# Attention beside a long convolution on one core: V projected in two halves of the heads, half-time transfers in four pieces, the last normalisation in two halves, later k chunks issued by SyncE

## The chip, the cores and the metric

The kernel runs on one core of a Trainium2 chip. The metric is the device time of one execution in microseconds (us); the times shown are of separate executions of the same program. The engines are TensorE (PE in the profile; PEld is its weight loads), VectorE (DVE), ScalarE (ACT), GpSimd (POOL) and SyncE (SP), which here only issues transfers.

## The reference

Two computations stand side by side in the output's 1024 columns. All tensors are bfloat16, the sequence has 2048 rows.

```python
# A: 32 heads of 16, columns 0..511 of the output
qkv = x @ wqkv                                   # [2048,512] @ [512,1536]
p   = softmax((q @ k^T) * 16**-0.5)              # no mask
a   = (p @ v).reshape(2048, 512) @ wo
# B: columns 512..1023
k_shift[s] = sum over t of k[s-3+t] * shift_k[:, 3-t]      # 4 taps
kv  = k_shift * v
y   = causal convolution of kv along s with ssm_k (2048 taps a channel) + kv * ssm_D
b   = q * y
```

## The kernel before, in words

**Attention.** Scores are made transposed, a block at a time: one block is one head strip, 128 keys by 512 queries. There are 2048 blocks: 4 query blocks `qb` x 8 groups `g` of four heads x 16 key tiles `kt` x 4 strips `s`. A step T takes a chunk of two or three blocks: TensorE makes them in two or three of six PSUM banks, three banks to even steps and three to odd ones (`emit_qk`, the L791 matmuls, K tile `KTo` and masked Q `QT`), ScalarE takes the exponential of the whole chunk in one instruction into `PT` (L798, 128x1024 for a pair, 128x1536 for a triple). In some triples the third block goes to VectorE instead (`exp_on_dve`: L817, a linear pass by GpSimd at L290, three passes at L826 and L827, result in `PTD`), and ScalarE then gets two blocks. Two steps later TensorE multiplies the exponentials with V (`emit_pv`, L866, four strips side by side). V lies in `VAF` with two columns of ones beside each head of 16, so that the sums come out with the product. After 64 blocks a group is done: `finish_group` transposes the PSUM bank on VectorE (L892), takes reciprocals (L899), multiplies (L901), and after every second group transposes back into `OTN` (L907). The output projection (`op_out`, L940) follows, 128 rows at a time.

**Projections.** x is transposed on TensorE (`turn_x`, L485), Q, K and V come from `pe_unit` (L507, L514, L521; a unit is four matmuls of 512 columns into one PSUM bank) and are copied out on VectorE by `evac_unit` (L542 for Q, L552 for K, L558 for V). In the first 70 steps the table `early` says at which step each unit comes; after that `units` does, by the group that needs the unit first (`next_unit`). A step with such a unit takes only two blocks, since the unit uses the third bank of its step. All 16 V units stand in `early`, all 32 heads at once, one key tile each.

**Convolution.** `kv_chunk` makes kv on VectorE for 256 rows at a time, chunk 7 first and chunk 0 last; `load_kv` fetches for each chunk v and four shifted copies of k (m = 0 to 3). v and m = 3 are issued by SyncE, m = 0, 1, 2 by GpSimd. Chunk 0 has rows before the sequence's start: GpSimd zeroes three partitions first (L424), and the shifted copies are fetched in two transfers each, the first of 127, 126 and 125 rows. When chunk 0 is done `start_conv` lets the convolution begin: 512 channels, four at a time (`qd`), 64 small matmuls for each four (`conv_lags`, L998), against a band matrix that SyncE fetches from a scratch buffer, 512 KB a channel, into a ring of 14 slots (`load_wr`). After each 32 channels `conv_turn` transposes back and multiplies by q in `QN`. `QN` holds 256 of the 512 channels: at half-time (after `conv_turn` 7) it is stored in one transfer of 1 MB and, 14 steps later, filled again with the second half of q in one transfer of 1 MB. Both are in SyncE's queue among the band matrices.

**What sets the order.** All engines run fixed streams of instructions, written when the program is built. A planner in Python keeps an estimated clock for each engine: PE's stream is written step by step (`emit_qk`, a unit, `emit_pv`, then early units or convolution up to an estimated limit), VectorE's from a list of jobs with due times (`dve_job`, `commit_one`), the transfers by estimated landing times (`landing`, `due_in`, `DMA_NS`). Matmuls with no result (`keep_busy`, `keep_zero`, `keep_active`: L1180, L1191, L1120) are put where the planner sees room and too little work in the past 3.4 us (`WINDOW`, `ACTIVE`). At run time each engine takes its stream in order and waits on semaphores.

**The end.** After the last exponential come the last L866, `finish_group`, four L940 into four banks, and `op_out_end`: ScalarE copies rows t = 1 and 3 and issues their stores, VectorE copies t = 0 and 2, whose stores SyncE issues.

## Time and profile before

| | |
|---|---|
| median of three executions | 843.6 us (839.74 to 861.82) |
| the profiled execution | 842.7 us |
| its span, first to last instruction | 840.8 us |
| mean granted TensorE clock | 0.993 |
| busy: ACT / DVE / PE / POOL | 818.2 / 797.5 / 710.1 / 283.7 us |
| moved by the DMA engines | 295.68 MB, 352 GB/s on average |

The profiled execution's own time is 1.9 us more than its span and 0.9 us below the median. A row of the timeline merges neighbouring instructions of one kind: start, length of the merged stretch, engine, line, count, and in brackets how long the engine stood idle before it and what ended that. SPq, ACTq and POOLq rows are the issuing of transfers. Two activations in a row overlap in the profile, so the mean length of one instruction is more than its share of the stretch.

### The profile page before, as it was taken

To read this page: it belongs to the slowest core of one execution; us is meant where nothing else is said; L and a number is where in the kernel's file an instruction comes from. 1 tells how busy PE (TensorE), PEld (TensorE's weight loads), DVE (VectorE), ACT (ScalarE), POOL (GpSimd) and SP (SyncE) were. 2 spreads that over 40 slices of the span, in tenths; PEclk is the share of its full clock that TensorE was granted. 3 is DMA by queue.
4 is the path that set the end of the run, shared out by engine and by line. 5 is a ranking of instruction groups with operands and counts; after the bars stand their busy time and mean duration, and the time that the engine had idled before them with its cause. 6 is when DMAs were issued, how large, how long until landed. Compare 5 with 4: busy or idle time off the path is not lost.

```text
span 840.8 us, 29871 instructions
## 1 busy us (share of the span) xinstructions
PE 710.1 (84%) x13098; PEld 310.1 (37%) x13144; DVE 797.5 (95%) x1346; ACT 818.2 (97%) x732; POOL 283.7 (34%) x307
## 2 busy tenths in 40 slices
PE   8988888888888888888888888788888888888887
PEld 3322333433333333333333334333333443333332
DVE  3998899999999999999999999999999999999996
ACT  6998999999999999999999999999999999999997
POOL 3232233333333333333332423333333333333331
PEclk9999999999999999999999999999999999999899
DMA  9878699999999999999998999999999999999810
GB/s 325 304 247 304 206 408 357 381 408 404 380 357 405 378 410 396 375 386 384 380 380 312 380 394 408 367 398 389 368 368 356 387 411 402 359 398 380 336 51 26
DMA packets 95778, 295.68 MB, mean 352 GB/s; under 512 B 11173, under 2 KB 27554, under 8 KB 95394
## 3 DMA queue, kind: packets, MB, share of 16 engines
q1 hardware_dynamic: 91266, 285.25, 89.5%
q0 software_dynamic: 2240, 7.34, 2.6%
q8 instruction: 105, 1.72, 0.8%
q10 hardware_dynamic: 2144, 1.18, 0.5%
q14 instruction: 23, 0.19, 0.1%
HBM read 287.31 MB, written 6.42 MB: 349 GB/s over the span
## 4 chain that ended last, share of the span: by engine, by line
ACT 72%; DVE 14%; PE 9%; issue 2%; DMA 1%; POOL 1%; ACTq 0%; DVEq 0%
ACT PT L798 72%; PE PS L791 3%; DVE EI L817 3%; DVE PTD L827 2%; DVE EM L826 2%; PE PS L866 2%; DVE WKV L826 2%; PE PS L521 1%; DMA WKV<-in_A_wqkv_dram 1%; PE PS L998 1%; DVE DT L892 1%; PE PS L507 1%; PE PS L514 1%; PE PS L940 1%; DMA QT<-in_B_k_dram 0%
## 5 line engine op out<-in xcount | busy, mean ns | idle before, releaser
L798 ACT ACTIVATE PT<-PS 128x1024 bf16<-128x1024 f32 (+1 forms) x726 | 814.6, 1338 | 11.1 <-PE PS L791 9.5
L791 PE MATMUL PS<-QT,KTo 32*128 32x512 bf16 x2048 | 286.5, 386 | 113.0 <-ACT PT L798 94.9
L998 PE MATMUL PS<-WR,KVP 128*30 128x128 bf16 (+15 forms) x8192 | 257.3, 221 | 2.7 <-issue 2.5
L290 POOL TENSOR_SCALAR EM<-EI 128x512 f32<-128x512 uint16 x131 | 129.2, 986 | 243.8 <-DVE WKV L826 122.4
L290 POOL TENSOR_SCALAR WKV<-EI 128x512 f32<-128x512 uint16 x130 | 128.2, 986 | 235.0 <-DVE EM L826 106.9
L998 PEld LDWEIGHTS PS<-WR,KVP 128*30 128x30 bf16 (+15 forms) x8192 | 177.9, 95 | 77.5 <-issue 37.7
L866 PE MATMUL PS<-PT,VAF 128*32 128x512 bf16 x1787 | 187.7, 392 | 1.3 <-DVE VAF L558 0.5
L817 DVE TENSOR_SCALAR EI<-PS 128x512 int32<-128x512 f32 x261 | 177.8, 681 | 3.4 <-PE PS L791 3.3
L826 DVE SCALAR_TENSOR_TENSOR EM<-EM 128x512 f32<-128x512 f32 x262 | 175.0, 683 | 1.8 <-POOL EM L290 1.5
L826 DVE SCALAR_TENSOR_TENSOR WKV<-WKV 128x512 f32<-128x512 f32 x260 | 173.1, 682 | 0.2
L791 PEld LDWEIGHTS PS<-QT,KTo 32*128 32x128 bf16 x2048 | 71.7, 91 | 274.7 <-ACT PT L798 223.8
L827 DVE SCALAR_TENSOR_TENSOR PTD<-EI,EM 128x512 uint16<-128x512 int32 x131 | 89.0, 680 | 0.4
L827 DVE SCALAR_TENSOR_TENSOR PTD<-EI,WKV 128x512 uint16<-128x512 int32 x130 | 88.1, 679 | 0.3
L866 PEld LDWEIGHTS PS<-PT,VAF 128*32 128x32 bf16 x1787 | 47.3, 93 | 106.7 <-issue 96.4
L866 PE MATMUL PS<-PTD,VAF 128*32 128x512 bf16 x261 | 78.5, 390 | 0.2
L1120 PE MATMUL PS<-IDN,ZER 128*32 128x512 bf16 x396 | 43.8, 380 | 0.0
L892 DVE STREAM_TRANSPOSE DT<-PS 128x512 f32<-128x512 f32 x31 | 22.2, 715 | 8.4 <-PE PS L866 8.1
L866 PEld LDWEIGHTS PS<-PTD,VAF 128*32 128x32 bf16 x261 | 19.8, 95 | 19.5 <-issue 8.6
L542 DVE TENSOR_TENSOR QT<-PS,MSK 128x1024 bf16<-128x1024 f32 x15 | 18.4, 1224 | 4.4 <-PE PS L507 4.3
L367 POOL DMA_DIRECT2D WR<-in_B_k_dram x15 | 11.0, 736 | 23.3 <-DVE KVP L618 14.7
L521 PE MATMUL PS<-WKV,xT 128*128 128x512 bf16 x58 | 17.8, 383 | 1.0 <-issue 0.8
L558 DVE CAST VAF<-PS 128x512 bf16<-128x512 f32 x16 | 11.0, 689 | 7.1 <-PE PS L521 7.1
(77 smaller groups left out, 272.3 us busy)
## 6 DMA issues: line engine op xcount, KB each, us to landing
WR<-kz_scratch SPq DMA_DIRECT2D x512, 512.0 KB, 7.9
WR<-in_B_k_dram POOLq DMA_DIRECT2D x15, 256.0 KB, 7.2
kz_scratch<-WR SPq DMA_DIRECT2D x4, 544.0 KB, 6.7
out_dram<-QN SPq DMA_DIRECT2D x2, 1024.0 KB, 7.5
QT<-in_B_k_dram POOLq DMA_DIRECT2D x7, 256.0 KB, 6.5
out_dram<-OUTA SPq DMA_DIRECT2D x12, 128.0 KB, 6.4
WR<-in_B_v_dram SPq DMA_DIRECT2D x5, 256.0 KB, 8.8
WR<-in_B_k_dram SPq DMA_DIRECT2D x5, 256.0 KB, 12.1
```

The costliest lines, as they stand in the source:

```text
L290: q.h = pool.op(lambda e: e.tensor_scalar(UB[m % len(UB)], f, PA, PB, ALU.mult, ALU.add), [h, fx.h, free], cost=Beside((h[0], h[1] + 1)))
L521: return e.matmul(PS[:, bank, :], lhsT=xT[:, dc, kt * 128:(kt + 1) * 128], rhs=WV[:, dc, :], start=(dc == 0), stop=(dc == 3))
L542: hh = dve_job(lambda e: e.tensor_tensor(QT[:, qb % 2, 2 * o:2 * o + 2, :], src, MSK[:, :, 0:1].broadcast_to([128, 2, QB]), ALU.mult), [h, ...
L791: ins = e.matmul(PS[:, bank, :], lhsT=KTo[32 * s:32 * s + 32, g // 2, kt * 128:(kt + 1) * 128], rhs=QT[32 * s:32 * s + 32, qb % 2, g, :], ...
L798: h_exp[T] = act.op(lambda e: e.activation(PT[:, T % R_PT, 0:n * QB], PS[:, banks[0]:banks[0] + n, :].rearrange("p b f -> p (b f)"), ACT.E ...
L817: h_fix[i] = job(lambda e: e.tensor_scalar(ei, PS[:, bank, :], FIX_LO, FIX_ADD, ALU.max, ALU.add), [h, h_pair.get(i - 4)], 692.0, end)
L826: js.append(job(lambda e, c=c: e.scalar_tensor_tensor(u, u, c, u, ALU.add, ALU.mult), [js[-1]], 693.0, due + 700.0 * (len(js) - 3)))
L827: js.append(job(lambda e: e.scalar_tensor_tensor(PTD[:, i % 4, :].bitcast(UINT16), ei, 2.0 ** -9, u, ALU.mult, ALU.add), [js[2], (lambda: ...
L866: ins = e.matmul(PS[32 * s:32 * s + 32, pvb(qb * NG + g), :], lhsT=VAF[:, kt, h * VW:h * VW + 32], rhs=rhs, start=first[b], stop=last[b], ...
L892: h_t = dve_job(lambda e: e.transpose(out=dt, in_=PS[:, pvb(n), :]), [h, h_mult.get(n - 2 if n == 2 else n - 1) if n != 1 else None], 717. ...
L998: ins = e.matmul(PS[32 * c:32 * c + m * NB - n, BGB, 128 * kk:128 * kk + 128], lhsT=KVP[:, o:o + 4 * (m * NB - n) - 3:4], rhs=WR[:, d % R_ ...
L1120: ins = e.matmul(PS[32 * s:32 * s + 32, pvb(n), :], lhsT=ZER[:, 0:32], rhs=IDN[:, :].rearrange("p (a f) -> p a f", a=1).broadcast_to([128, ...
```

## The change

- **V in halves.** A V unit now covers two key tiles and half of the heads: eight matmuls of 256 columns instead of four of 512, one copy of the same size. `VAF` holds the two halves of a key tile 304 columns apart. The weights come in two transfers; the second half's go into `OUTA`, which is free until the first output projection (whose copy now waits for the last V matmul). Of the 16 units, the eight of the first half and two of the second stand in `early`, six of the second in `units`; the K units (1,2) and (1,3) go from `units` into `early`.
- **Fill.** `keep_busy` reads the identity instead of `VAF`, so it can run from the start, and its bound in the early steps is `EARLY_ACTIVE` 6000 instead of 4800.
- **Half-time in pieces.** The store of `QN` and its refilling become four transfers of 256 KB each, four steps apart, and the planner charges 1000 ns for each instead of 8000 ns in one place.
- **Last normalisation in halves.** `finish_half` does columns 0 to 255 through all its passes, then 256 to 511. In `op_out_end` ScalarE copies t = 0, 1, 3 and VectorE t = 2; SyncE issues the stores of t = 0, 1, 2.
- **k chunks by SyncE.** For chunks 4 to 0 all of k is issued by SyncE. The zeroed area of chunk 0 is half as large. The planner reckons chunk 0's landing 3 us later.

```diff
+VHALF = 304
+VROW = 2 * VHALF
+EARLY_ACTIVE = 6000.0
+KV0_NS = 6600.0
+QN_STEPS = 4
+QN_NS = 1000.0
...
-    WV = WKV[:, 1, :, :]
+    WV = [WKV[:, 1, :, 0:256], OUTA[:, 0:2, :].rearrange("p a (b d) -> p (a b) d", d=256)]
...
-    h_wv = landing(dma(act, d_w[2], WV, wview[:, :, 2 * D:3 * D]), 8.5)
+    h_wv = [landing(dma(act, d_w[2], WV[0], wview[:, :, 2 * D:2 * D + 256]), 8.5)]
...
+    h_wv.append(landing(dma(act, d_w[5], WV[1], wview[:, :, 2 * D + 256:3 * D]), 14.5))
...
-            z = QT[0:3, 1, 2:8, :]
+            z = QT[0:3, 1, 2:8:2, :]
...
-            q = sp if m == 3 else pool
+            q = sp if m == 3 or j < 5 else pool
...
-            due_in(h_kv[(j, 0)], at_of(deps[0] if deps[0] and j else h_kvfree[2] if not j else h_edge), 3600.0)
+            due_in(h_kv[(j, 0)], at_of(deps[0] if deps[0] and j else h_kvfree[2] if not j else h_edge), 3600.0 if j else KV0_NS)
...
+            _, f, i = u
+            deps += h_x[i // 2] + [h_wv[f]]
...
             def mm(e, dc):
-                return e.matmul(PS[:, bank, :], lhsT=xT[:, dc, kt * 128:(kt + 1) * 128], rhs=WV[:, dc, :],
-                                start=(dc == 0), stop=(dc == 3))
+                for c in (2 * dc % 4, 2 * dc % 4 + 1):
+                    kt = 2 * i + dc // 2
+                    ins = e.matmul(PS[:, bank, 256 * (dc // 2):256 * (dc // 2) + 256], lhsT=xT[:, c, kt * 128:(kt + 1) * 128],
+                                   rhs=WV[f][:, c, :], start=(c == 0), stop=(c == 3))
...
+    def finish_half(p, c, h):
+        cols = slice(256 * c, 256 * c + 256)
+        dt, dtn = DT[:, cols], DTN[:, p % 2, cols]
+        h_t = dve_job(lambda e: e.transpose(out=dt, in_=PS[:, pvb(n), cols]), [h, h_mult[n - 1]], 400.0, 300.0 + c)
...
+        h_r = dve_job(lambda e: e.reciprocal(rcp, blocks[:, :, DH:DH + 1]), [h_t], 170.0, 0.0)
...
+        for i in range(2):
+            t = 2 * c + i
+            h_otn[(p, t + 1)] = h_otn[p] = dve_job(
+                lambda e, t=t: e.transpose(out=OTN[:, oslot(n), 128 * t:128 * t + 128], in_=DTN[:, p % 2, 128 * t:128 * t + 128]),
...
+        if last:
+            for c in range(2):
+                finish_half(p, c, h)
+            return
...
-        if t % 2:
+        if t != 2:
             hh = act.op(lambda e: e.activation(dst, PS[:, bank, :], ACT.Copy), [h], cost=515.0)
...
-        dma(act if t % 2 else sp, d_outE, out2[r0:r0 + 128, 0:D], dst, [hh])
+        dma(act if t == 3 else sp, d_outE, out2[r0:r0 + 128, 0:D], dst, [hh])
...
-            ho = dma(sp, d_outB[0], dst, QN[:, :, :], [hh])
-            if sl == 0:
-                dve_later.append((len(chunks) + 14, lambda: load_qn(1, [ho], 0, NB)))
+            def part(i):
+                ho[i] = dma(sp, d_outB[i], dst[:, 4 * i:4 * i + 4, :], QN[:, 4 * i:4 * i + 4, :], [hh])
+                later_row(QN_NS)
+            def again(i):
+                load_qn(1, [ho[i]], 4 * i, 4 * i + 4, i == 3)
+                later_row(QN_NS)
...
-    early = {1: ("v", 0), 3: ("v", 1), 5: ("t", 3), 6: ("v", 2), 8: ("t", 2), 9: ("v", 3), 10: ("k", 0, 1),
+    early = [(0, ("r",)), (1, ("v", 0, 0)), (2, ("x", 1, 0)), (4, ("x", 1, 1)), (6, ("t", 3)), (7, ("v", 0, 1)), (9, ("t", 2)),
...
-    units = [(2 + 8 / 16, ("k", 1, 2)), (2 + 12 / 16, ("k", 1, 3))]
+    units = []
...
+    units += [(4 + i / 8, ("v", 1, i)) for i in range(2, 8)]
...
-            ins = e.matmul(PS[:, bank, :], lhsT=IDN[:, :], rhs=VAF[:, 0, 0:512], start=True, stop=True)
+            ins = e.matmul(PS[:, bank, :], lhsT=IDN[:, :], rhs=IDN[:, :].rearrange("p (a f) -> p a f", a=1).broadcast_to([128, 4, 128]),
+                           start=True, stop=True)
```

Three places show what moves. First TensorE's stream some ten steps into the program, before. QT,KTo is a chunk's scores, WKV,xT half a V unit, PT,VAF the product with V, IDN,KVP a transposition of x, IDN,SHK a spread of the shift taps:

```order
L791 MATMUL PS<-QT,KTo 128x512 x2
L866 MATMUL PS<-PT,VAF 32x512 x4
L485 MATMUL PS<-IDN,KVP 128x128 x8
L791 MATMUL PS<-QT,KTo 128x512 x2
L521 MATMUL PS<-WKV,xT 128x512 x2
L791 MATMUL PS<-QT,KTo 128x512 x2
L866 MATMUL PS<-PT,VAF 32x512 x4
L521 MATMUL PS<-WKV,xT 128x512 x2
L791 MATMUL PS<-QT,KTo 128x512 x2
L485 MATMUL PS<-IDN,KVP 128x128 x8
```

The same place of the changed kernel, where L806 is the scores, L881 the product with V, L492 x, L583 the taps, and L1229 a fill pair:

```order
L806 MATMUL PS<-QT,KTo 128x512 x2
L881 MATMUL PS<-PT,VAF 32x512 x4
L492 MATMUL PS<-IDN,KVP 128x128 x8
L806 MATMUL PS<-QT,KTo 128x512 x2
L492 MATMUL PS<-IDN,KVP 128x128 x8
L806 MATMUL PS<-QT,KTo 128x512 x2
L881 MATMUL PS<-PT,VAF 32x512 x4
L1229 MATMUL PS<-IDN 128x512 x2
L806 MATMUL PS<-QT,KTo 128x512 x2
L583 MATMUL PS<-IDN,SHK 128x128 x4
```

The third and fourth V halves have left this stretch, the second transposition of x has moved up, and a fill pair stands in between.

Second, SyncE's queue at half-time, before (WR<-kz_scratch are band matrices, QN the q and result buffer, OUTA rows of the attention's output):

```order
L367 DMA WR<-kz_scratch 128x2048 x132
L367 DMA out_dram<-QN 128x16x256
L367 DMA out_dram<-OUTA 128x512 x2
L367 DMA WR<-kz_scratch 128x2048 x4
L367 DMA out_dram<-OUTA 128x512
L367 DMA QN<-in_B_q_dram 128x16x256
L367 DMA WR<-kz_scratch 128x2048 x4
```

And in the changed kernel:

```order
L372 DMA out_dram<-QN 128x4x256
L372 DMA out_dram<-OUTA 128x512
L372 DMA out_dram<-QN 128x4x256
L372 DMA WR<-kz_scratch 128x2048 x4
L372 DMA out_dram<-QN 128x4x256
L372 DMA WR<-kz_scratch 128x2048 x4
L372 DMA QN<-in_B_q_dram 128x4x256
L372 DMA WR<-kz_scratch 128x2048 x4
L372 DMA QN<-in_B_q_dram 128x4x256 x2
L372 DMA WR<-kz_scratch 128x2048 x4
L372 DMA QN<-in_B_q_dram 128x4x256
```

The 2 MB now stand in eight pieces (the first store is three rows further up), with four band matrices between most of them.

Third, VectorE's last instructions, before:

```order
L892 STREAM_TRANSPOSE DT<-PS 128x512
L899 RECIPROCAL DR<-DT 128x16
L901 TENSOR_TENSOR DTN<-DT,DR 128x16x16
L907 STREAM_TRANSPOSE OTN<-DTN 128x128 x4
L961 CAST QT<-PS 128x512 x2
```

And in the changed kernel:

```order
L906 STREAM_TRANSPOSE DT<-PS 128x256
L909 RECIPROCAL DR<-DT 128x8
L911 TENSOR_TENSOR DTN<-DT,DR 128x8x16
L916 STREAM_TRANSPOSE OTN<-DTN 128x128 x2
L906 STREAM_TRANSPOSE DT<-PS 128x256
L909 RECIPROCAL DR<-DT 128x8
L911 TENSOR_TENSOR DTN<-DT,DR 128x8x16
L916 STREAM_TRANSPOSE OTN<-DTN 128x128 x2
L993 CAST QT<-PS 128x512
```

Three instructions more, each of half the size, and one copy of the output less.

Over the whole program ScalarE's pairs and triples go from 391 and 335 to 396 and 332, VectorE's own blocks from 261 to 260, and the fill pairs that stand ahead of the convolution's first matmul from 9 to 20.

85 lines of the change are left out of this document (51 added, 34 removed), and 8 rows, old and new, of the table early.

## The prediction

> **What bounds the kernel now.** I read the page's first part, then the chain that ended last, then ScalarE by form and in order of time. The busy shares and the chain's shares:
>
> ```profile
> PE 710.1 (84%) x13098; PEld 310.1 (37%) x13144; DVE 797.5 (95%) x1346; ACT 818.2 (97%) x732; POOL 283.7 (34%) x307
> ...
> ACT 72%; DVE 14%; PE 9%; issue 2%; DMA 1%; POOL 1%; ACTq 0%; DVEq 0%
> ```
>
> ScalarE is busy for 97% of the span and carries 72% of the chain. VectorE is close behind, so it is a second bound wherever its stream blocks at its head. ScalarE's exponentials by form, first in the whole span and then in the quiet stretch from 285 to 455.3 us:
>
> ```profile
> L798 ACT ACTIVATE PT<-PS 128x1536 bf16<-128x1536 f32 x335 | 513.0, 1577 | 5.6 <-PE PS L791 5.3
> L798 ACT ACTIVATE PT<-PS 128x1024 bf16<-128x1024 f32 x391 | 425.4, 1134 | 5.5 <-PE PS L791 4.2
> ```
>
> ```profile
> L798 ACT ACTIVATE PT<-PS 128x1536 bf16<-128x1536 f32 x79 | 123.6, 1619 | 0.3 <-PE PS L791 0.3
> L798 ACT ACTIVATE PT<-PS 128x1024 bf16<-128x1024 f32 x70 | 82.2, 1207 | 0.0
> ```
>
> And ScalarE in order of time, merged stretches from the first exponential to the last:
>
> ```profile
> 8.94 4.01 ACT L798 ACTIVATE PT<-PS 128x1024 bf16<-128x1024 f32 x4 [0.74 <-PE PS L791]
> 13.60 34.71 ACT L798 ACTIVATE PT<-PS 128x1024 bf16<-128x1024 f32 x36 [0.66 <-PE PS L791]
> 48.48 22.63 ACT L798 ACTIVATE PT<-PS 128x1024 bf16<-128x1024 f32 x24 [0.17 <-PE PS L791]
> 72.06 7.92 ACT L798 ACTIVATE PT<-PS 128x1024 bf16<-128x1024 f32 x8 [0.95 <-PE PS L791]
> 80.97 6.40 ACT L798 ACTIVATE PT<-PS 128x1536 bf16<-128x1536 f32 x5 [0.99 <-PE PS L791]
> ...
> 284.83 170.54 ACT L798 ACTIVATE PT<-PS 128x1536 bf16<-128x1536 f32 x149 [0.28 <-PE PS L791]
> ...
> 810.79 23.14 ACT L798 ACTIVATE PT<-PS 128x1536 bf16<-128x1536 f32 x21 [0.18 <-PE PS L791]
> ```
>
> A triple costs 1577 - 1134 = 443 ns more than a pair. The quiet stretch holds 149 in 170.54 us, so a pair takes (170.54 - 79 x 0.443) / 149 = 0.910 us and a triple 1.353 us. All exponentials at these prices are 391 x 0.910 + 335 x 1.353 = 809.1 us. They run from 8.94 to 810.79 + 23.14 = 833.93, which is 825.0 us. So **15.9 us of the stream are lost**; 8.9 us lie ahead of it and 6.9 behind. The largest loss is early: 72 pairs from 8.94 to 80.97 take 72.0 us against 72 x 0.910 = 65.5, that is 6.5 us. No edit to the order can bring more than these 15.9 us and a part of the ends, so 2% (16.9 us, about what a measurement of this kernel can tell from no change) is out of reach on the fast side.
>
> **The change part by part.**
>
> *ScalarE's own work.* Five pairs more and three triples fewer: 5 x 0.910 - 3 x 1.353 = **+0.5 us**.
>
> *V out of the early stage.* Three of the four early gaps (0.66, 0.95, 0.99) come from TensorE's stream waiting on VectorE:
>
> ```profile
> 12.29 0.40 PE L866 MATMUL PS<-PT,VAF 128*32 128x512 bf16 x4 [0.47 <-DVE VAF L558]
> ...
> 71.63 0.39 PE L791 MATMUL PS<-QT,KTo 32*128 32x512 bf16 x2 [1.26 <-DVE QT L542]
> ...
> 80.53 0.40 PE L791 MATMUL PS<-QT,KTo 32*128 32x512 bf16 x3 [0.65 <-DVE KTo L552]
> ```
>
> ```profile
> L558 DVE CAST VAF<-PS 128x512 bf16<-128x512 f32 x16 | 11.0, 689 | 7.1 <-PE PS L521 7.1
> ```
>
> Sixteen V copies take 11.0 us of VectorE, which stands 7.1 us blocked ahead of them. With six of them gone, VectorE gets 6 x 0.69 + 7.1 x 6/16 = 6.8 us of room in 72 us. TensorE gains nothing in volume: six units of 2048 columns leave, and eleven more fill pairs of 1024 come, so its work there falls only by 12288 - 11264 = 1024 columns. I take the three gaps as gone, 0.66 + 0.95 + 0.99 = **-2.6 us**, and leave the other 3.9 us of the early loss. Bounds: nothing recovered and a new gap of the largest size seen there, +1.0, to all of it, -6.5. The value stands between, at the gaps that VectorE ends, because it is VectorE that gets the room. A matmul of 256 columns has no row here; if eight of them cost a quarter more than four of 512, that lies in the pairs' slack or adds within the same bound.
>
> *V in the later stage.* Six V units come in and two K units leave, four units net. Their matmuls and copies lie beside the exponentials, and their pairs are already counted. The row at 284.83 shows what such a step costs when its copy is late: a gap of 0.28 us. Bounds 0 and 6 x 0.28 = 1.7; I take **+0.3 us**, one gap, as most such steps in the trace show none.
>
> *Half-time in pieces.* Two stretches of 20 us around it, and three others; the columns are busy time of PE, PEld, DVE, ACT and POOL with counts, granted clock, DMA share and GB/s:
>
> ```profile
> 20.00:40.00 20.00, 19.52 (x137) 6.06 (x138) 17.67 (x31) 19.50 (x22) 4.33 (x6) 1.00 0.87 301
> ...
> 440.00:460.00 20.00, 16.32 (x232) 6.41 (x232) 19.47 (x34) 19.72 (x18) 5.59 (x7) 1.00 0.87 321
> 460.00:480.00 20.00, 16.39 (x350) 7.67 (x348) 18.89 (x32) 18.81 (x18) 7.36 (x8) 1.00 1.04 364
> ...
> 600.00:620.00 20.00, 16.17 (x320) 6.80 (x321) 17.79 (x31) 18.60 (x17) 6.61 (x7) 0.91 1.00 376
> ...
> 780.00:800.00 20.00, 17.81 (x346) 7.76 (x350) 18.91 (x33) 19.03 (x18) 7.17 (x8) 0.83 0.82 316
> ```
>
> From 440 to 460 TensorE does 232 matmuls instead of some 350: the convolution is held back while 2 MB pass. Then from 440 to 480 ScalarE is idle for 0.28 + 1.19 = 1.5 us. Part of this has no cause that the profile names:
>
> ```profile
> PE PS L998 <- issue: 2.5, 2, 1.2
> ```
>
> Twice TensorE stands 1.2 us for no visible reason, once here, and this I can't credit. I take half of the 1.5, **-0.8 us**. Bounds: all of it, -1.5, and the other way +1.5, if pieces of 256 KB that wait in SyncE's queue for their own stores hold up the band matrices behind them.
>
> *k chunks by SyncE.* Chunk 0 is the one that VectorE waits for:
>
> ```profile
> 74.23 2.65 POOL L424 MEMSET QT<- 3x3072 bf16 x1 [13.32 <-DVE KVP L618]
> 77.18 2.94 POOL L367 DMA_DIRECT2D QT<-in_B_k_dram  x5 [0.30 <-POOL QT L424]
> ...
> 76.91 0.38 SPq L367 DMA_DIRECT2D QN<-in_B_v_dram  x1
> 77.34 1.47 SPq L367 DMA_DIRECT2D QT<-in_B_k_dram  x2
> ...
> 83.68 0.69 DVE L598 TENSOR_TENSOR QT<-QT,WR 128x1024 bf16<-128x1024 bf16 x1 [1.30 <-DMA QT<-in_B_k_dram]
> ```
>
> Half the area zeroed saves 2.65 / 2 = 1.3 us. But SyncE now issues eight transfers in a row, at 1.47 / 2 = 0.74 us, where two queues shared them: about 0.4 + 7 x 0.74 = 5.5 us against GpSimd's 2.94 + 0.3, so 2.3 us later. Net the chunk lands 1.0 us later. The planner now puts VectorE's first work on it 3 us later, which covers that; VectorE does V copies there instead. I take **0**. Bounds: -1.3, if the whole wait of VectorE goes, to +3, below among the rivals. GpSimd's freed time is worth nothing, as it is busy for 34%. Chunks 4 to 1 move three issues each to SyncE, 2.2 us in front of at most ten band matrices that are needed only after chunk 0.
>
> *The end.*
>
> ```profile
> 834.42 0.72 DVE L892 STREAM_TRANSPOSE DT<-PS 128x512 f32<-128x512 f32 x1 [3.96 <-PE PS L866]
> ...
> 835.17 0.25 DVE L899 RECIPROCAL DR<-DT 128x16 f32<-128x16 f32 x1
> 835.46 0.43 DVE L901 TENSOR_TENSOR DTN<-DT,DR 128x256 bf16<-128x256 f32 x1
> 835.92 0.89 DVE L907 STREAM_TRANSPOSE OTN<-DTN 128x128 bf16<-128x128 bf16 x4
> 836.28 1.04 PE L940 MATMUL PS<-WKV,OTN 128*128 128x512 bf16 x4 [1.16 <-DVE OTN L907]
> ...
> 836.93 0.60 ACT L959 ACTIVATE QT<-PS 128x512 bf16<-128x512 f32 x1 [3.00 <-PE PS L940]
> ...
> 837.97 0.60 ACT L959 ACTIVATE QT<-PS 128x512 bf16<-128x512 f32 x1 [0.44 <-ACT QT L959]
> ```
>
> A half costs about 0.39 + 0.20 + 0.24 + 0.44 and gaps of 0.16, 1.43 us. The last row tile is thus ready at 834.42 + 2 x 1.43 = 837.3, not 836.81, but the first is ready at 835.6 instead of 836.2. ScalarE copies t = 0 and 1 while VectorE does the second half, and copies t = 3 from 837.3 + 0.35 = 837.65 instead of 837.97; its own store no longer stands between two copies. **-0.3 us**, bounds -0.9 and +0.3 (VectorE's copy of t = 2 is behind all its halves).
>
> The sum: 0.5 - 2.6 + 0.3 - 0.8 + 0 - 0.3 = -2.9. The profiled execution took 842.7 us, so **839.8 us**; that execution lies 0.9 us under the median of 843.6, well within the spread of the three runs.
>
> **The rivals.**
>
> *The early stage gains nothing.* The stage is TensorE's (19.52 us busy of 20 from 20 to 40), and the fill pairs take what V leaves. For it: the volume is the same within 1024 columns. Against it: the gaps end on VectorE. Then -2.6 falls away: 842.4 us, no change.
>
> *Chunk 0 comes late.* From 460 to 480 the 16 engines moved 364 GB/s, 23 GB/s each. If the 127 rows of 1 KB that SyncE now issues went through one engine, they would take 5.7 us and hold VectorE until about 3 us later than planned, as everything behind that wait stands in VectorE's stream. It would give 839.8 + 3 = 842.8 us. The Trainium skill, DMA: Bandwidth & Descriptors, section "Why a DMA increments its semaphore by 16 and not by 1", says just this: a transfer issued by SyncE is spread over the largest number of engines up to 16 that divides its rows, and 127 rows get one engine. By that rule the 842.8 is the time; the trace before has only the 125 rows of m = 3 on SyncE, and shows no landing for them.
>
> *TensorE's clock drops more often: slower than before.* In the two stretches at 0.91 and 0.83 ScalarE lost 1.4 and 1.0 us. The missing clock is 0.09 x 20 and 0.17 x 20 us, 5.2 us in all, so a lost microsecond of clock costs about 0.5 us. The change draws convolution work and fills into other places; if the late stage falls under the activity that keeps the clock, it decides from 6 us of lost clock more than now, and 12 us more would give 839.8 + 6 = 846 us. The Trainium skill, TensorE: Matmul & The Clock Gate, section "Part 1: The HAM clock gate", has the clock at either half or full by windows of 3.4 us; the two stretches fit it, as half clock through one window and through two would read 0.91 and 0.83. One execution at 861.82 shows that the same program can lose 19 us more. Against it: the matmuls without result rise in number rather than fall.
>
> **How the numbers follow.** The forecast has 0.60 (834 to 843.5 with its own bounds). An early stage that recovers nearly all, 833 to 835, has 0.06; one that recovers nothing 0.13; a late chunk 0 has 0.09; the clock 0.12, of which half ends above 2%. The range of 832 to 850 leaves out the last and little else. Faster by over 2% would need a time below 826.7, past all losses: 0.02. Slower, above 860.5: 0.06. Within: 0.92.
>
> **What would show it.** Right: the three early gaps on ScalarE are gone and the first 70 pairs end near 8.94 + 70 x 0.910 + 3.9 = 76.5 us; at half-time no 20 us have as few as 232 matmuls; ScalarE's last copy starts near 3.7 us after the last exponential. VectorE's wait for chunk 0 stays under 1.5 us. Wrong: a wait of TensorE on a V copy or on a band matrix, a wait of VectorE on chunk 0 of 3 us or more, or more than two stretches of 20 us under a clock of 0.95.

## The result, and the profile after

| | before | after |
|---|---|---|
| median (lowest to highest, executions) | 842.77 us (838.61 to 861.82, 7) | 848.26 us (845.93 to 850.5, 7) |
| ratio, with its 95% interval | | 1.0076 (1.0052 to 1.0101) |
| the profiled execution, and its span | 842.7 us, 840.8 | 846.81 us, 845.1 |
| mean granted clock of the profiled execution | 0.993 | 0.992 |

The change made the kernel 0.8% slower, where 0.3% faster (2.9 us) was forecast. The time lies in the forecast's range, but on the wrong side of the time before. Executions over 1.5% above the fastest of the same kernel, such as the one of 861.82 us, are left out of every ratio and of the fit below.

ScalarE in order of time shows first what came as forecast, then what did not:

```profile
8.94 3.93 ACT L813 ACTIVATE PT<-PS 128x1024 bf16<-128x1024 f32 x4 [0.74 <-PE PS L806]
13.48 74.05 ACT L813 ACTIVATE PT<-PS 128x1024 bf16<-128x1024 f32 x75 [0.61 <-PE PS L806]
92.76 2.96 ACT L813 ACTIVATE PT<-PS 128x1536 bf16<-128x1536 f32 x2 [5.24 <-PE PS L806]
96.32 1.02 ACT L813 ACTIVATE PT<-PS 128x1024 bf16<-128x1024 f32 x1 [0.60 <-PE PS L806]
...
829.33 8.62 ACT L813 ACTIVATE PT<-PS 128x1024 bf16<-128x1024 f32 x9 [0.15 <-PE PS L806]
...
841.92 0.60 ACT L991 ACTIVATE QT<-PS 128x512 bf16<-128x512 f32 x1 [0.57 <-PE PS L972]
```

Of the four early gaps one is left, 0.61. The merged stretch that starts at 13.48 holds seven triples among its 75, so 72 pairs and seven triples end at 87.53: 78.59 us against 72 x 0.910 + 7 x 1.353 = 75.0. The early loss is 3.6 us, where it was 6.5, and the first 70 pairs end at 76.29, near the 76.5 of the forecast. Then comes a gap of 5.24 us that the trace before does not have. Three rows of the waits lead back through it, in the order total, times, longest:

```profile
ACT PT L813 <- PE PS L806: 14.0, 17, 5.2
...
PE PS L806 <- DVE QT L556: 9.0, 9, 5.3
...
DVE QT L613 <- DMA QT<-in_B_k_dram: 5.9, 1, 5.9
```

ScalarE waits for scores, TensorE for a copy of Q that VectorE makes (L556), and VectorE stands at the head of its stream before its first work on chunk 0 (L613) until the shifted copies of k have landed. In order of time, VectorE's last row ahead of the wait, the wait, and the copy of Q behind it:

```profile
82.88 0.71 DVE L943 STREAM_TRANSPOSE OTN<-DTN 128x512 bf16<-128x512 bf16 x1
89.53 1.29 DVE L613 TENSOR_TENSOR QT<-QT,WR 128x1024 bf16<-128x1024 bf16 x2 [5.94 <-DMA QT<-in_B_k_dram]
90.74 1.22 DVE L556 TENSOR_TENSOR QT<-PS,MSK 128x1024 bf16<-128x1024 f32 x1
```

Before, the same work began at 83.68 after a wait of 1.30 us, so chunk 0 is ready 5.85 us later. TensorE's rows around its idle time:

```profile
85.32 0.39 PE L806 MATMUL PS<-QT,KTo 32*128 32x512 bf16 x3
...
92.11 0.61 PE L806 MATMUL PS<-QT,KTo 32*128 32x512 bf16 x3 [5.31 <-DVE QT L556]
```

The same score matmuls take 0.39 us before the idle time and 0.61 behind it. The row of that stretch, in the columns of the prediction's tables, gives the clock that goes with it, and the three rows of half-time:

```profile
80.00:100.00 20.00, 14.27 (x83) 3.29 (x82) 10.61 (x19) 12.77 (x12) 0.00 (x0) 0.83 0.38 119
```

```profile
440.00:460.00 20.00, 17.01 (x334) 7.57 (x326) 19.90 (x34) 20.00 (x19) 6.67 (x7) 1.00 1.02 378
460.00:480.00 20.00, 17.18 (x335) 8.06 (x336) 19.45 (x33) 19.77 (x19) 5.68 (x6) 1.00 0.98 353
480.00:500.00 20.00, 16.62 (x304) 6.96 (x309) 19.59 (x34) 20.00 (x18) 6.94 (x7) 1.00 1.05 400
```

From 80 to 100 the granted clock is 0.83, where it was 1.00. The half-time transfers now lie from 468 to 500 us, where they began at 445 before. From 440 to 500 ScalarE is idle for 0.2 us, where it was 1.5 from 440 to 480 before, and none of the three stretches has as few as 232 matmuls, as forecast. Of the signs of being wrong two came: VectorE's wait of over 3 us, and waits of TensorE on a V copy, 0.6 us at most.

### The profile page after: what moved, and what is told of

Same layout as the page of the kernel before. It is cut to its first block, busy times and chain, and to the rows that moved or that the text cites. A ratio compares the mean times of both kernels' runs of the same rounds, so it can differ in the third digit from the quotient of the medians.

```text
span 845.1 us, 30058 instructions
## 1 busy us (share of the span) xinstructions
PE 714.0 (84%) x13192; PEld 316.7 (37%) x13232; DVE 795.6 (94%) x1344; ACT 818.5 (97%) x735; POOL 269.2 (32%) x291
## 4 chain that ended last, share of the span: by engine, by line
ACT 75%; PE 12%; DVE 10%; issue 1%; DMA 1%; SPq 1%; POOL 0%; DVEq 0%
ACT PT L813 75%; PE PS L806 4%; PE PS L881 2%; DVE EI L832 2%; DVE EM L841 2%; DVE WKV L841 2%; DVE PTD L842 2%; PE PS L531 1%; PE PS L514 1%; PE PS L1229 1%; DMA QT<-in_B_k_dram 1%; PE PS L1032 1%; DVE QT L556 1%; SPq L372 1%; PE PS L972 1%
## 5 line engine op out<-in xcount | busy, mean ns | idle before, releaser
L813 ACT ACTIVATE PT<-PS 128x1536 bf16<-128x1536 f32 (+1 forms) x728 | 814.4, 1352 | 15.3 <-PE PS L806 14.0
L806 PE MATMUL PS<-QT,KTo 32*128 32x512 bf16 x2048 | 287.5, 386 | 114.9 <-ACT PT L813 92.0
L1032 PE MATMUL PS<-WR,KVP 128*22 128x128 bf16 (+16 forms) x8192 | 251.4, 221 | 2.0 <-issue 1.7
L1032 PEld LDWEIGHTS PS<-WR,KVP 128*26 128x26 bf16 (+15 forms) x8192 | 174.8, 95 | 77.4 <-issue 39.5
L295 POOL TENSOR_SCALAR EM<-EI 128x512 f32<-128x512 uint16 x130 | 127.3, 979 | 231.1 <-DVE WKV L841 104.6
L881 PE MATMUL PS<-PT,VAF 128*32 128x512 bf16 x1788 | 185.5, 391 | 1.7 <-issue 0.6
L806 PEld LDWEIGHTS PS<-QT,KTo 32*128 32x128 bf16 x2048 | 71.6, 91 | 272.9 <-ACT PT L813 218.1
L881 PEld LDWEIGHTS PS<-PT,VAF 128*32 128x32 bf16 x1788 | 46.9, 93 | 105.8 <-issue 99.4
L881 PE MATMUL PS<-PTD,VAF 128*32 128x512 bf16 x260 | 77.5, 382 | 0.0
L881 PEld LDWEIGHTS PS<-PTD,VAF 128*32 128x32 bf16 x260 | 19.7, 94 | 16.2 <-issue 7.0
L556 DVE TENSOR_TENSOR QT<-PS,MSK 128x1024 bf16<-128x1024 f32 x15 | 18.4, 1224 | 5.2 <-PE PS L514 5.0
L972 PE MATMUL PS<-WKV,OTN 128*128 128x512 bf16 x50 | 14.5, 381 | 3.4 <-DVE OTN L916 1.5
L1229 PE MATMUL PS<-IDN 128*128 128x512 bf16 x54 | 17.2, 401 | 0.0
L566 DVE CAST KTo<-PS 128x512 bf16<-128x512 f32 x15 | 10.3, 689 | 6.4 <-PE PS L521 6.1
```

The source lines that it names most:

```text
L295: q.h = pool.op(lambda e: e.tensor_scalar(UB[m % len(UB)], f, PA, PB, ALU.mult, ALU.add), [h, fx.h, free], cost=Beside((h[0], h[1] + 1)))
L556: hh = dve_job(lambda e: e.tensor_tensor(QT[:, qb % 2, 2 * o:2 * o + 2, :], src, MSK[:, :, 0:1].broadcast_to([128, 2, QB]), ALU.mult), [h, ...
L806: ins = e.matmul(PS[:, bank, :], lhsT=KTo[32 * s:32 * s + 32, g // 2, kt * 128:(kt + 1) * 128], rhs=QT[32 * s:32 * s + 32, qb % 2, g, :], ...
L813: h_exp[T] = act.op(lambda e: e.activation(PT[:, T % R_PT, 0:n * QB], PS[:, banks[0]:banks[0] + n, :].rearrange("p b f -> p (b f)"), ACT.E ...
L881: ins = e.matmul(PS[32 * s:32 * s + 32, pvb(qb * NG + g), :], lhsT=VAF[:, kt, VHALF * (h // 16) + h % 16 * VW:VHALF * (h // 16) + h % 16 * ...
L972: ins = e.matmul(PS[:, bank, :], lhsT=OTN[:, (4 * qb + j) % R_O, t * 128:(t + 1) * 128], rhs=WOP[:, j, :], start=(j == 0), stop=(j == 3))
```

## The experiments

Twelve runs follow, one of them a second trace of a kernel. The times move with the clock that TensorE was granted: the executions of one kernel that differ in time differ in mean clock too. One line with a common slope, and a level of its own for each kernel, fitted through 221 executions gives 0.58 us for each 0.001 of mean clock, with a scatter of 1.1 us about it. The last column is each kernel's level at a clock of 0.995, to about 0.7 us either way (0.2 for the kernel before, 0.9 for the one after, 1.0 for before_chunk0_on_sync). It is meant to separate what a kernel does from how often its clock dropped; that all kernels share one slope is an assumption. Each ratio compares means, with executions of the kernel before that were made beside it.

| kernel | median, us | ratio to before, 95% | mean clock | at 0.995, us |
|---|---|---|---|---|
| before (96 executions) | 842.1 | | 0.993 | 841.7 |
| after | 848.3 | 1.0076 (1.0052 to 1.0101) | 0.989 | 844.7 |
| chunk0_on_gpsimd | 840.8 | 0.999 (0.996 to 1.002) | 0.994 | 840.7 |
| chunk0_split_112 | 841.9 | 0.9985 (0.9962 to 1.0009) | 0.993 | 840.6 |
| split_127_only | 841.8 | 0.9991 (0.9968 to 1.0013) | 0.994 | 840.8 |
| before_chunk0_on_sync | 848.3 | 1.0054 (1.0018 to 1.009) | 0.992 | 846.9 |
| cut_113 | 846.4 | 1.0042 (1.002 to 1.0064) | 0.992 | 844.8 |
| split_112_norm_whole | 840.1 | 0.9973 (0.9952 to 0.9994) | 0.994 | 840.3 |
| split_112_tail_as_before | 841.2 | 0.9981 (0.9957 to 1.0005) | 0.995 | 840.7 |
| split_112_half_whole | 843.8 | 1.0011 (0.9988 to 1.0035) | 0.992 | 842.3 |
| split_112_v_as_before | 845.0 | 1.003 (1.0002 to 1.0058) | 0.990 | 841.7 |
| v_halves_alone | 845.3 | 1.0027 (1.0001 to 1.0053) | 0.992 | 843.7 |
| v_halves_due_later | 845.5 | 1.0032 (1.0002 to 1.0061) | 0.992 | 843.1 |

### Chunk 0's transfers

**The kernel after, with chunk 0's three copies back on GpSimd** (chunks 4 to 1 stay with SyncE):

```diff
-            q = sp if m == 3 or j < 5 else pool
+            q = sp if m == 3 or 0 < j < 5 else pool
```

> The changed kernel with the m = 0, 1, 2 copies of chunk 0 issued by GpSimd again; all else, and every other engine's order, is unchanged. Theory (127 rows issued by SyncE go through one DMA engine and hold VectorE 5.9 us): VectorE's wait on chunk 0 falls from 5.9 to under 1.5 us, ScalarE's 5.24 us gap goes with the 0.6 and 1.3 behind it, and the time falls from 848 by 7 to 10 us to 838 to 841. Rival A (eight issues one after another in SyncE's queue make it late): the same, as the issues are shared again. Rival B (the loss is V units in the later stage or a clock that drops by itself): less than 3 us change, 845 to 849.

```profile
83.05 1.29 DVE L613 TENSOR_TENSOR QT<-QT,WR 128x1024 bf16<-128x1024 bf16 x2 [0.42 <-DMA QT<-in_B_k_dram]
```

VectorE's wait is 0.42 us and the median 840.8. With chunk 0's three copies back in GpSimd's queue the whole loss is gone, although chunks 4 to 1 still come from SyncE.

**The kernel after, with each uneven transfer cut into 112 rows and the rest**, all still issued by SyncE:

```diff
-                h = dma(q, ds, b[m][m:128, 0, :], k2[0:128 - m, :], deps)
+                dma(q, ds, b[m][m:m + 112, 0, :], k2[0:112, :], deps)
+                h = dma(q, ds, b[m][m + 112:128, 0, :], k2[112:128 - m, :], deps)
```

> The changed kernel with the transfers of 127, 126 and 125 rows each cut into 112 rows and the rest, all still in SyncE's queue: three issues more, and no transfer that has to go through one engine. Theory (one engine): VectorE's wait on chunk 0 falls under 2 us and the time to 838 to 842. Rival A (the number of issues in one queue): three issues more at 0.85 us make the wait 8.5 us, and the time 850 or more. Rival B: 845 to 849, no change.

The wait for chunk 0 and the 20 us around it:

```profile
84.52 1.29 DVE L614 TENSOR_TENSOR QT<-QT,WR 128x1024 bf16<-128x1024 bf16 x2 [0.92 <-DMA QT<-in_B_k_dram]
```

```profile
80.00:100.00 20.00, 18.43 (x187) 6.37 (x185) 17.08 (x30) 19.47 (x18) 4.10 (x5) 1.00 0.48 159
```

Three issues more in the same queue, and the chunk is ready 5 us sooner. A queue that is late by the number of its issues cannot do that. The median is 841.9. Three more kernels below keep these transfers and V in halves, and their waits are 0.78, 1.08 and 1.31 us: by so much the wait differs from one trace to the next.

**Only the 127-row transfer cut**, at 112:

```diff
+                n = 112 if m == 1 else 0
+                if n:
+                    dma(q, ds, b[m][m:m + n, 0, :], k2[0:n, :], deps)
+                h = dma(q, ds, b[m][m + n:128, 0, :], k2[n:128 - m, :], deps)
```

> The changed kernel with only the 127-row transfer cut, into 112 and 15 rows; the 126 and 125 rows stay whole. Theory (127 rows alone go through one engine; 126 and 125 divide by 14 and 5): nearly all of the wait goes, to under 2.5 us, 839 to 843. Rival A (issues): 0.85 us more wait, 848 to 850. If uneven rows as such were slow, half of the wait would stay: 843 to 846.

```profile
84.85 1.29 DVE L616 TENSOR_TENSOR QT<-QT,WR 128x1024 bf16<-128x1024 bf16 x2 [1.86 <-DMA QT<-in_B_k_dram]
```

The wait is 1.86 us, the median 841.8: this one transfer holds 4.1 of the 5.0 us that the three cuts take away.

**The same cut at 113 rows:**

```diff
-                n = 112 if m == 1 else 0
+                n = 113 if m == 1 else 0
```

> Only the 127-row transfer of chunk 0 is cut, as in split_127_only, but at 113 rows instead of 112: 113 is a prime and 112 is 7 x 16. Queue, number of issues and bytes are the same. One-engine theory (a SyncE transfer uses the largest number of engines up to 16 that divides its rows): 113 rows still go through one engine, some 203 KB on the fullest engine instead of 217, so VectorE's wait for chunk 0 stays above 4.5 us (5.9 less 0.6) and the time stays at 846.5 to 848.5 us. Rival (any cut helps, because a shorter transfer lets the next ones start, or because the queue's order changes): as split_127_only, a wait near 1.9 us and 841 to 843 us.

```profile
89.15 1.29 DVE L616 TENSOR_TENSOR QT<-QT,WR 128x1024 bf16<-128x1024 bf16 x2 [5.56 <-DMA QT<-in_B_k_dram]
```

The delay is back, 5.56 us, and so is most of the time, 846.4, just under the 846.5 to 848.5 of the one-engine theory. Queue, number of issues and bytes are those of split_127_only. What differs is that 112 has the divisor 16 and 113 has none but itself. The issuing shows it too: SyncE needs 3.55 us for its eight k transfers of chunk 0 with 112 rows and 5.01 with 113; the ten of chunk0_split_112 take 4.56.

The packets of the whole program bear on how many engines each transfer used; after, cut_113, split_127_only and chunk0_split_112 in this order:

```profile
DMA packets 99263, 295.69 MB, mean 350 GB/s; under 512 B 11268, under 2 KB 31998, under 8 KB 98878
DMA packets 99277, 295.69 MB, mean 350 GB/s; under 512 B 11282, under 2 KB 32012, under 8 KB 98892
DMA packets 99293, 295.69 MB, mean 352 GB/s; under 512 B 11298, under 2 KB 32028, under 8 KB 98908
DMA packets 99333, 295.69 MB, mean 353 GB/s; under 512 B 11338, under 2 KB 32068, under 8 KB 98948
```

The bytes are the same, and all that is added are packets under 512 B (of 4 bytes each, in the traces): 14, 30 and 70 more than after. Suppose that every engine which a transfer uses adds one such packet. Then with 127, 126 and 125 rows on 1, 14 and 5 engines (20 in all), 113 + 14 on 1 + 14, 112 + 15 on 16 + 15, 112 + 14 on 16 + 14 and 112 + 13 on 16 + 13, the sums are 20, 34, 50 and 90, and their differences are just these 14, 30 and 70.

**The kernel before, with chunk 0's copies issued by SyncE** and nothing else:

```diff
-            q = sp if m == 3 else pool
+            q = sp if m == 3 or j == 0 else pool
```

> The kernel before with this one part alone: all of chunk 0 issued by SyncE, the area zeroed, the planner's landing time and every other engine's order as before. Theory: the wait of VectorE on chunk 0 grows from 1.3 to 6 to 9 us (same transfers, and the planner's order begins 3 us earlier), and the time goes up from 842.8 by 4 to 8 us to 847 to 851. Rival B: within 2 us of before.

```profile
89.91 0.69 DVE L598 TENSOR_TENSOR QT<-QT,WR 128x1024 bf16<-128x1024 bf16 x1 [7.67 <-DMA QT<-in_B_k_dram]
```

This line alone brings about as large a loss as the change: 848.3 us, a ratio of 1.0054 (1.0018 to 1.009). Here the planner puts VectorE at chunk 0 earlier (82.24 us instead of 83.59), so the wait is longer.

### The other parts, without the late chunk

These start from chunk0_split_112 and undo one part each, or do V's part alone.

**The last normalisation whole again** (`finish_half` is not called, the code of before does the last group):

```diff
-        if last:
-            for c in range(2):
-                finish_half(p, c, h)
-            return
...
-        if dyn[0]:
+        if last:
+            mult()
+            for i in range(4):
+                turn_back(i, i + 1)
+        elif dyn[0]:
```

> As chunk0_split_112, with the last normalisation whole again; ScalarE still copies three of the last four row tiles. That kernel has 7.3 us from the end of the last exponential to the end of the span, the kernel before 6.9. Theory (halves cost more instructions on VectorE than the earlier start of the first row tiles gives back): the tail falls to 6.6 to 6.9 us and the time by 0.4 to 0.7, to 841.2 to 841.5. The forecast's step (halves bring 0.3): the tail grows to 7.6 and the time to 842.2.

**And the copies of the last row tiles as before too:**

```diff
-        if t != 2:
+        if t % 2:
...
-        dma(act if t == 3 else sp, d_outE, out2[r0:r0 + 128, 0:D], dst, [hh])
+        dma(act if t % 2 else sp, d_outE, out2[r0:r0 + 128, 0:D], dst, [hh])
```

> As split_112_norm_whole, with the copies of the last four row tiles too as before (ScalarE t = 1 and 3, VectorE 0 and 2, stores from both queues). From the end of the last exponential to the end of the span split_112_norm_whole has 7.24 us and the kernel before 6.87. Theory (the copies moved to ScalarE, and with them a third store on SyncE's queue, cost the 0.3 to 0.4): the tail is 6.8 to 6.95, the time 839.8. Rival (the end of the last store differs from one execution to the next): 7.1 to 7.4, and the time 840.1.

From the end of the last exponential to the end of the span, split_112_norm_whole takes 7.2 us and chunk0_split_112 7.3, so the theory that the halves cost 0.4 to 0.7 falls, and the forecast's 7.6 without them does not come either. With the whole end as before it is longer still. Its last rows:

```profile
821.48 8.61 ACT L814 ACTIVATE PT<-PS 128x1024 bf16<-128x1024 f32 x9 [0.15 <-PE PS L807]
833.09 0.60 ACT L992 ACTIVATE QT<-PS 128x512 bf16<-128x512 f32 x1 [3.00 <-PE PS L973]
833.72 0.37 ACTq L372 DMA_DIRECT2D out_dram<-QT  x1
834.14 0.60 ACT L992 ACTIVATE QT<-PS 128x512 bf16<-128x512 f32 x1 [0.45 <-ACT QT L992]
834.76 0.36 ACTq L372 DMA_DIRECT2D out_dram<-QT  x1
```

The last exponential ends at 830.09 and the span at 837.6, 7.5 us later; the kernel before, with the same instructions, took 6.9. Up to the end of ScalarE's last issue the two agree (5.03 and 5.02 us). From there to the end of the span it is 2.5 against 1.85 us. That last piece, behind every instruction of these engines, differs between two traces of the same ending by twice what the whole step was said to bring. The part up to the last issue repeats to 0.01 us (4.96 after and 4.97 in chunk0_split_112, with the same ending) and tells the two edits apart: 5.03 us with the end as before, 4.75 with the copies moved (split_112_norm_whole), 4.97 with the halves as well (chunk0_split_112). The moved copies bring 0.3 there and the halves take 0.2 of it back.

**The half-time transfers whole again** (the code of before, with the 8000 ns of the planner):

```diff
-            for i in range(4):
-                dve_later.append((now + QN_STEPS * i, lambda i=i: part(i)))
-                dve_later.append((now + QN_STEPS * (i + 4), lambda i=i: again(i)))
+            ho = dma(sp, d_outB[0], dst, QN[:, :, :], [hh])
+            if sl == 0:
+                dve_later.append((len(chunks) + 14, lambda: load_qn(1, [ho], 0, NB)))
```

With it goes back a line in `next_unit` that the change had altered too: how soon a `conv_turn` is due once all channels are done.

> As chunk0_split_112, with the half-time transfers whole again, and the planner's 8 us for them. Theory (the pieces do what the forecast said): from 440 to 480 ScalarE is idle 1.2 to 1.5 us again, one stretch of 20 us there has some 230 matmuls instead of over 300, and the time is 842.5 to 843.5. Rival (the pieces bring nothing, the 1.2 us of TensorE there come from elsewhere): the idle time there stays under 0.5 us or shows up unchanged at another place, time 841.5 to 842.2.

```profile
440.00:460.00 20.00, 17.19 (x313) 7.49 (x313) 19.63 (x35) 20.00 (x19) 7.67 (x8) 1.00 1.00 373
460.00:480.00 20.00, 16.83 (x318) 7.11 (x314) 19.77 (x34) 19.91 (x19) 5.92 (x6) 1.00 1.03 344
480.00:500.00 20.00, 16.98 (x341) 7.33 (x325) 19.50 (x33) 20.00 (x19) 7.91 (x8) 1.00 1.03 364
```

The time of 843.8 is a little above the 842.5 to 843.5 that the theory gave, and not by its mechanism: the two transfers are issued at 460.56 and 478.63, ScalarE is idle for 0.1 us there, and the convolution is not held back. In this trace, of an execution of 847.33 us, one loss lies later, at a place where TensorE stands with no cause that the profile names, and then gets a clock of 0.62 from 648 to 652 us:

```profile
647.52 0.55 PE L807 MATMUL PS<-QT,KTo 32*128 32x512 bf16 x3 [3.05 <-issue]
648.00 0.50 PE L1033 MATMUL PS<-WR,KVP 128*12 128x128 bf16 x12
```

The trace of v_halves_alone, which has whole transfers too, has such a stop ahead of the same line, 2.50 us at 652.84; the trace of v_halves_due_later does not. So at equal clock this kernel is 1.7 us slower than with the pieces, give or take 1, and where that comes from stays open.

**V and the fill as before**, the rest of the change kept (with it go back the tables `early` and `units`, the copies and `EARLY_ACTIVE`):

```diff
-    WV = [WKV[:, 1, :, 0:256], OUTA[:, 0:2, :].rearrange("p a (b d) -> p (a b) d", d=256)]
+    WV = WKV[:, 1, :, :]
...
-            _, f, i = u
-            deps += h_x[i // 2] + [h_wv[f]]
+            _, kt = u
+            deps += h_x[kt // 4] + [h_wv]
```

> The kernel before with k by SyncE (cut at 112 rows), half-time in pieces and the tail in halves: all of the change but the V halves and their fill. Early loss is the time from the first exponential to some 95 us less the pairs at 0.910 and triples at 1.353; later loss that from 95 to 125 us. chunk0_split_112 has 4.0 and 2.6. Theory (V in halves gains 3 early and gives 2 back where its second half is copied): early loss 6 to 7 with the three gaps back, later loss under 1, and the time 842 to 843.5. Forecast's terms (early -2.6, later +0.3): time 844 to 845. A rival in which V in halves is worth nothing or costs: 841.9 or less.

The median is 845.0, 3.1 us more than chunk0_split_112, near the forecast's terms. Its trace shows the early gaps again (0.66 and 0.95 us on ScalarE; at half clock the third can't be told apart), and behind the one at 71 us a clock of 0.58, 0.50 and 0.50:

```profile
69.88 0.40 PE L870 MATMUL PS<-PT,VAF 128*32 128x512 bf16 x4
71.53 0.39 PE L795 MATMUL PS<-QT,KTo 32*128 32x512 bf16 x2 [1.26 <-DVE QT L546]
```

```profile
68.00:72.00 4.00, 2.74 (x21) 0.84 (x20) 3.96 (x7) 3.05 (x5) 0.00 (x0) 1.00 1.01 312
72.00:76.00 4.00, 4.00 (x16) 0.68 (x14) 3.83 (x8) 2.92 (x3) 1.37 (x1) 0.58 0.50 203
76.00:80.00 4.00, 4.00 (x18) 0.69 (x16) 0.60 (x1) 2.11 (x3) 0.00 (x0) 0.50 0.76 226
80.00:84.00 4.00, 4.00 (x14) 0.92 (x11) 3.19 (x6) 2.60 (x3) 0.00 (x0) 0.50 0.36 104
```

**A second trace of the same kernel:**

> The same kernel as split_112_v_as_before, a second look at its trace. There TensorE stood 1.26 us ahead of L795 at 71.5 us and ran at half clock from 72.7 to about 86; the kernel before shows the same 1.26 us and no drop. If the drop comes with this kernel's fixed order, it is there again. If the same order of work sits at the edge of what keeps the clock, it may be gone, with a time 4 to 6 us shorter than a run with it.

```profile
71.50 0.39 PE L795 MATMUL PS<-QT,KTo 32*128 32x512 bf16 x2 [1.26 <-DVE QT L546]
```

```profile
68.00:72.00 4.00, 2.64 (x18) 0.82 (x19) 3.96 (x7) 3.05 (x5) 0.00 (x0) 1.00 0.86 291
72.00:76.00 4.00, 3.95 (x24) 1.01 (x24) 3.81 (x8) 3.81 (x4) 1.37 (x1) 1.00 0.67 271
```

The same stream stands for the same 1.26 us at the same place, and the clock stays at 1.00. This execution took 840.14 us, the first one 848.04. The kernel's 13 executions run from 839.04 us at a mean clock of 0.997 to 850.6 at 0.982.

**V's part alone, in the kernel before.** To it come the V halves, the tables `early` and `units` and the fill of the change's diff; half-time, end and chunk 0 stay. Against split_112_tail_as_before, besides the whole half-time transfers and the line of `next_unit` named above:

```diff
-            z = QT[0:3, 1, 2:8:2, :]
+            z = QT[0:3, 1, 2:8, :]
...
-            q = sp if m == 3 or j < 5 else pool
+            q = sp if m == 3 else pool
...
-                dma(q, ds, b[m][m:m + 112, 0, :], k2[0:112, :], deps)
-                h = dma(q, ds, b[m][m + 112:128, 0, :], k2[112:128 - m, :], deps)
+                h = dma(q, ds, b[m][m:128, 0, :], k2[0:128 - m, :], deps)
...
-KV0_NS = 6600.0
+KV0_NS = 3600.0
```

> The kernel before with V in halves and the fill that goes with it, and nothing else of the change: chunk 0 by GpSimd, half-time transfers whole, the end as before. The kernel before has a median of 842.1 beside it, and an early loss with three gaps of 0.7 to 1.0 us on ScalarE before 81 us. Forecast's terms (0.5 more of ScalarE's work, -2.6 early, +0.3 later): 840.3. Theory that the later stage gives back 2 (V copies at 95 to 125 us, with gaps that end on them): 841.5 to 842.1, no gain. If what split_112_v_as_before lost is all V's, 839. In each case the three early gaps are gone.

None of the three numbers came: the median is 845.3. The early gaps are gone as every theory said, but VectorE stands 3.14 us ahead of chunk 0 instead of 1.30. It gets there only 0.2 us sooner (82.18 against 82.38); chunk 0 is ready 1.6 us later (85.32 against 83.68). GpSimd's zeroing, with which chunk 0 begins, starts at 75.82 instead of 74.23: it waits for VectorE's product for an earlier chunk (L633, `KVP`), and VectorE's order ahead of that has changed, with two V copies in it, at 71.20 and 74.40. Behind VectorE's wait TensorE stands, and its clock drops, in this trace. GpSimd's row, VectorE's, TensorE's and the 20 us around them:

```profile
75.82 2.65 POOL L430 MEMSET QT<- 3x3072 bf16 x1 [13.97 <-DVE KVP L633]
```

```profile
85.32 0.69 DVE L613 TENSOR_TENSOR QT<-QT,WR 128x1024 bf16<-128x1024 bf16 x1 [3.14 <-DMA QT<-in_B_k_dram]
```

```profile
88.56 0.61 PE L806 MATMUL PS<-QT,KTo 32*128 32x512 bf16 x3 [1.76 <-DVE QT L556]
```

```profile
80.00:100.00 20.00, 17.77 (x116) 4.62 (x114) 12.73 (x23) 16.01 (x15) 3.96 (x7) 0.83 0.53 177
```

**The same with the later due time for chunk 0:**

```diff
-KV0_NS = 3600.0
+KV0_NS = 6600.0
```

> As v_halves_alone, with the change's later due time for chunk 0 (6.6 us instead of 3.6) and nothing else. In v_halves_alone VectorE reached chunk 0 3.14 us before it had landed, TensorE stood 1.76 us and its clock read 0.83 from 80 to 100 us. Theory (V in halves needs the later due time, since fewer V copies let VectorE come to chunk 0 sooner): VectorE's wait falls below 1 us, the clock from 80 to 100 reads 1.00, and the time falls by 2 to 3, to 842.3 to 843.5; the whole half-time transfers are still in it. Forecast's terms for V alone: 840.3. Rival (the due time is nothing, the loss of v_halves_alone is that of a late stage): the wait falls and the time stays at 845.

The wait falls to 1.6 us, not below 1, and the clock from 80 to 100 us reads 1.00 in this trace. Chunk 0 is as late as in v_halves_alone (85.21); only VectorE now comes later, at 83.57. The median stays, 845.5, as the rival had it. At equal clock it is 0.6 us better, less than the uncertainty of 0.9. So the due time is not what V's part alone lacks, and the theory falls. The three kernels with V in halves and whole half-time transfers are slower than before at equal clock: v_halves_alone by 2.0 us and v_halves_due_later by 1.4, and split_112_half_whole by 0.6, which is less than its uncertainty.

## Why the prediction was wrong, step by step

**k chunks by SyncE: the step that failed.** It was put at 0, with the chunk landing 1.0 us later inside the planner's 3 us. It landed 5.85 us later. The step reckoned 5.5 us for SyncE's eight issues and let a transfer's landing be the same from either queue. The eight took 6.36 us, and the chunk landed 5.97 us after the last of them, where it had been 3.56 after GpSimd's last. The 1.3 us credited for the smaller zeroed area did not come either: the zeroing took 1.37 us instead of 2.65, but began at 75.81 instead of 74.23, as in v_halves_alone. The rival of the late chunk had the mechanism and got 0.09. Its price of 3 us was too small as well, because it took the 127 rows by themselves. By the rule that it cited (the Trainium skill, DMA: Bandwidth & Descriptors, "Why a DMA increments its semaphore by 16 and not by 1": a transfer that SyncE issues is spread over the largest number of engines up to 16 that divides its rows), and counting engines from the same first one for each transfer, which is an assumption, the chunk's KB on the fullest engine can be set beside VectorE's wait:

| kernel | rows of the first transfers | engines | KB on the fullest engine | wait, us |
|---|---|---|---|---|
| after | 127, 126, 125 | 1, 14, 5 | 127 + 9 + 25 + 56 = 217 | 5.94 |
| cut_113 | 113 + 14, 126, 125 | 1, 14, 14, 5 | 113 + 1 + 9 + 25 + 56 = 204 | 5.56 |
| split_127_only | 112 + 15, 126, 125 | 16, 15, 14, 5 | 7 + 1 + 9 + 25 + 56 = 98 | 1.86 |
| chunk0_split_112 | 112 + 15, 14, 13 | 16, 15, 14, 13 | 3 x (7 + 1) + 56 = 80 | 0.92 |

The 56 are the chunk's even transfers, 16 KB each for two of 256 KB and 8 for each of three of 128. From the first row to the last, 137 KB bring 5.0 us, some 27 KB a microsecond and engine, against the 23 that the prediction took from 364 GB/s; with the last row's wait anywhere from 0.78 to 1.31 us it is 27 to 30. The trace agrees with the rule: the number of small packets differs by just what the column of engines asks for, and the pair of 112 and 113 rows is its test in time. Where GpSimd issues the same 127 and 126 rows the list of transfers (chunk0_on_gpsimd) shows them landed in 4.1 and 3.8 us:

```profile
QT<-in_B_k_dram POOLq DMA_DIRECT2D x1, 127.0 KB, 4.1
QT<-in_B_k_dram POOLq DMA_DIRECT2D x1, 126.0 KB, 3.8
```

**TensorE's clock.** This rival was held to be a way of its own, with 0.12. It came as a consequence: TensorE's 5.31 us of idle time were followed by half clock (0.50 from 92 to 96 us), and the mean clock of the seven executions after is 0.989 against 0.993. Of the 5.5 us between the means of the fit's executions (848.2 and 842.7), 3.0 are there at equal clock and 2.5 are the clock's (0.0044 x 580). Against chunk0_split_112 the late chunk costs 844.7 - 840.6 = 4.1 at equal clock and 2.2 by the clock. The rival's price of 0.5 us for each microsecond of lost clock was a little small: 0.001 of an 845 us span is 0.845 us of clock, and it costs 0.58 us, 0.7 for each.

**V out of the early stage: right in the gaps, the reckoning behind them incomplete.** The three gaps went, and the loss fell by 2.9 us against 2.6 forecast. But the third gap had ended on the K copies at 79.7 us, and the change also puts their units, (1,2) and (1,3), into `early`, which the step left out: they are now copied at 65.2 and 67.2 us. So V's room need not be what closed that gap; no run separates the two. What was not forecast is that one of these gaps is a place where the clock can drop, as the two traces of one kernel show.

**V in the later stage: mis-sized.** 0.3 was forecast. In chunk0_split_112 16 pairs and eight triples take from 95.62 to 123.57, 27.95 us, against 25.4 by their prices: 2.6 us are lost, where the kernel before loses next to nothing there. The price of 0.28 was read off a gap at 284.83 where no copy was late: TensorE's scores at 284.40 in the trace before follow a Q unit's matmuls and an L866 without a pause. TensorE's waits in the stretch from 95 us end on the V copies that moved, and on a K copy between them:

```profile
96.45 0.39 PE L807 MATMUL PS<-QT,KTo 32*128 32x512 bf16 x3 [0.54 <-DVE VAF L573]
100.65 0.49 PE L807 MATMUL PS<-QT,KTo 32*128 32x512 bf16 x3 [0.24 <-DVE VAF L573]
118.44 0.40 PE L807 MATMUL PS<-QT,KTo 32*128 32x512 bf16 x3 [0.88 <-DVE KTo L567]
```

Taken at equal clock, V in halves is worth 1.1 us (841.7 - 840.6), give or take 1, where 1.8 was forecast; by the medians, with the clock that it spares, 3.1.

**ScalarE's own work: right.** The kernel has 396 pairs and 332 triples, +0.5 us.

**Half-time in pieces: the sign right, the reason not borne out.** The idle time at half-time went as forecast, but it is gone in the new order with whole transfers too, so the pieces were not needed for that. The 1.7 us between the two kernels is measured; its cause is open.

**The end: not -0.3.** The time from the last exponential to the end of ScalarE's last issue fell from 5.02 to 4.96 us, and ScalarE's last copy starts 3.97 us after the last exponential, where 3.7 was forecast and 4.04 measured before. The step credited the halves and the moved copies together; up to the last issue the copies bring 0.3 and the halves take 0.2 back. Behind the last issue the traces differ by more than that.

**The sum.** Without the late chunk the change is about what the other steps said, at the small end: the five kernels that keep V in halves and the pieces are at 840.1 to 841.9 us, with ratios from 0.9973 (0.9952 to 0.9994) to 0.9991 (0.9968 to 1.0013), 0.1 to 0.3% under before where 0.3% (2.9 us) was forecast. At equal clock it is 0.9 to 1.4 us. split_112_norm_whole is the only kernel whose interval lies wholly below the one before. The parts do not add up: at equal clock all other parts with V as before give 0, V in halves with whole transfers costs 0.6 to 2.0, and all together gain 1.1, each to about 0.7 us. Each part moves the order of all that the planner writes behind it, which no sum of terms held.
